# The first low word of each pair's weight sums on VectorE, and layer two's first two rows taking the sixth block together

## The chip, the core and the metric

The kernel runs on one core of a Trainium2 chip. Five engines work side by side, each through its own instructions in a fixed order: PE (TensorE, the matrix multiplications), DVE (VectorE), ACT (ScalarE), POOL (GpSimd) and SP (SyncE, which issues the transfers). An instruction that waits holds up all that stand behind it on its engine. The metric is the device time in microseconds; lower is better.

## What is computed

A block-sparse attention feeds two feed-forward layers over 1536 tokens of width 512:

```python
x = attention(q, k, v)                                # (1536, 512)
h = np.maximum(np.maximum(x @ w1, x @ w2), x @ w3)    # w1..w3: (512, 768)
y = h @ w_out                                         # layer two
out = ((y @ w_a) * (y @ w_b)) @ w_out2                # layers three and four, inner width 1536
```

## The kernel before

**Numbers in two words.** Each fp32 operand of a large product is held as a high and a low word: ACT rounds it to the high word (L464 for weights, L536 for data), and another engine subtracts that from the original to get the low word (L465, L537). A product then takes three matrix multiplications (`mm3`, L529 to L533): high by high, low by high, high by low, all 128 x 128 by 384 tokens.

**Chunks and stages.** The tokens are four chunks of 384 (c = 0 to 3). Chunks 0 and 1 go through layers one and two while the attention still runs. Chunks 2 and 3 go through layer one in `pair1`: the first two and the last of its nine steps are plain products (`plain`, names `ph`), and the six between are computed for both chunks at once by seven block products in place of eight (`products`, names `hb`, `hg`, `hd`). That scheme needs sums of weight blocks, which `w_sums` (L613) makes for a pair (f, m): POOL adds high and low word back together (L614, `rc`), DVE forms four sums in `sums4` (L471 to L474, `s12` and `s34`), and both go through `w_parts`, where ACT makes the high and one engine the low word. Before, POOL makes both low words, since `LO_G` is True. Layer two (`layer2`, names `py`) multiplies the six blocks f of h by one weight column block m for each of four rows of y. Layers three and four follow (`qb`, `qg`, `qd`, then `po`); the first products of layer three are the start of `layer3` for `order34[0]` and `order34[1]`.

**PSUM.** The products from `pair1` on share a ring of eight PSUM banks (tag "r"). A bank is taken again only when its last reader has read it, and within the seven products a bank that has been read for an intermediate result is added to afterwards, so that PE also waits for these readers: `result` (L631: DVE L633, L635, L640, ACT L638 and L684) and, in layer three, DVE L803 and L809 (`ca`, `t`) and ACT L793.

**Weights of layers three and four.** Their 512 KB pieces are loaded by SP into three buffers (`w64`). The first three loads are held back by a one-column copy on POOL (L433). From each piece ACT makes two parts (L454 into `psw` or in place, L456), DVE puts the fp32 number together (L458, L459, `w32`), POOL adds the last bits (L460), and then come the sums and splits as above (L471 to L474, L464, L465). A piece's POOL instruction frees its buffer for the next load.

**What sets the order.** The Python code says what depends on what and in which order it is written; a planner then places each engine's instructions by its own estimate of when they can run. A change in the code moves instructions on several engines, far from the lines that were edited.

Of the kernel before, what the change touches and what calls it, by code (L numbers as in the profile page):

```python
# [19 lines left out]
P = 128  # L20
# [16 lines left out]
NCH, MAXT = len(CHUNKS), max(SIZES)  # L37
# [5 lines left out]
N1, N2, NK = 3 * FF1 // P, FF1 // P, FF2 // P // 3  # L43
# [16 lines left out]


GATE, ROOM, SUMS, EARLY34 = (2, 1), 16, (40, 43, 46, 49), 6
PLAIN, XSUMS, WSUMS, WS, PT, MAX_G, LO_G, ASK = (2, 1), (2, 4), (5, 7), 8, 7, False, True, (0, 2)
RING, LEAD, TURN, ERA0, ASKS, AHEAD, PRE, TURNS = 8, 5, (11, 2, 4), 10, (3, 4, 5, 7, 9), (4, 1), 3, ((6, N1 - 6, 6, 4, 4), (24, 34), (34, 43))


# [11 lines left out]
def attention_then_maxout_then_bilinear(ctx: ExitStack, tc: tile.TileContext, qt, kt, vt, vwin, wall, const, out):  # L78
# [4 lines left out]
    V, A, G, T = nc.vector, nc.scalar, nc.gpsimd, nc.tensor  # L83
# [339 lines left out]
    w64_t, w32_t, w_t = {}, {}, {}  # L423
# [38 lines left out]
    def w_parts(r, eng, tag="w34", n=512):  # L462
        w = w_p.tile([P, 2, n], F32R, tag=tag, name="wt", bufs=2 if n < 512 else WS if tag == "ws" else WBUFS[tag != "w"])
        A.activation(w[:, 0], r, AF.Copy)  # L464
        eng.tensor_tensor(w[:, 1], r, w[:, 0], ALU.subtract)  # L465
        return w

    def sums4(a11, a12, a21, a22):

        s12, s34 = (w32_p.tile([P, 512], F32, tag=f"s{i}", name="s", bufs=1) for i in range(2))  # L470
        V.tensor_tensor(s12[:, 0:256], a21, a22, ALU.add)  # L471
        V.tensor_tensor(s12[:, 256:512], s12[:, 0:256], a11, ALU.subtract)
        V.tensor_tensor(s34[:, 0:256], a11, a21, ALU.subtract)
        V.tensor_tensor(s34[:, 256:512], a12, s12[:, 256:512], ALU.subtract)  # L474
        return s12, s34
# [37 lines left out]
    late = []  # L513

    def flush():
        while late:
            late.pop(0)()

    def bank(name):

        return ps_m.tile([P, 512], F32, tag="m", name=name)
# [7 lines left out]
    def mm3(ps, w, o, x, first, last, more=False):  # L529

        for n, (i, j) in enumerate(((0, 0), (1, 0), (0, 1))):
            ins = T.matmul(ps, w[:, i, o:o + P], x[:, j], start=first and n == 0, stop=last and n == 2, skip_group_check=more).ins  # L532
        return ins  # L533
# [10 lines left out]
    def layers12(c):  # L544

        n_, hs, pend = CHUNKS[c][2] * P, {}, [None]
        for n in range(N1):
            f, m = divmod(n, 3)
            if m == 0:
                hs[f] = hg_p.tile([P, 2, MAXT * P], F32R, tag="hg", name="hg")  # L550
            ps = bank("ph")[:, 0:n_]
            for k in range(4):
                mm3(ps, w_t[n], k * P, x_t[c, k], k == 0, k == 3)
            flush()

            def evac(f=f, m=m, ps=ps, ht=hs[f]):
                prev, pend[0] = pend[0], temp(f"t{m}", c)
                if m == 0:
                    mark[1] = A.activation(pend[0], ps, AF.Copy).ins
                else:  # L560
                    mark[0] = V.tensor_tensor(pend[0], ps, prev, ALU.max).ins
                    if m == 2:
                        split(ht, pend[0], G)

            late.append(evac)
            yield
        yield from layer2(c, hs, bank)

    def layer2(c, hs, bank):

        ys[c] = y_p.tile([P, 4, MAXT * P], F32, tag="y", name="y", bufs=NCH)
        for m in range(4):
            ps = bank("py")[:, 0:MAXT * P]
            for f in range(N2):
                if m == 0 and f == N2 - 1:
                    flush()
                mm3(ps, w_t[N1 + f], m * P, hs[f], f == 0, f == N2 - 1)
            flush()
            late.append(lambda m=m, ps=ps: halves(c, m, ps))
            yield  # L580

    xs = {}

# [25 lines left out]
    def w_sums(f, m):  # L609

        w0, w1 = (w_t[3 * (f + i) + m] for i in range(2))
        r0, r1 = (w32_p.tile([P, 512], F32, tag="rc", name="rc", bufs=2) for _ in range(2))
        for r, w in ((r0, w0), (r1, w1)):  # L613
            G.tensor_tensor(r, w[:, 0], w[:, 1], ALU.add)  # L614
        s12, s34 = sums4(*(r[:, o:o + 256] for r in (r0, r1) for o in (0, 256)))
        eng = G if LO_G else V
        s12, s34 = (w_parts(x, eng, "ws") for x in (s12, s34))
        w_s[f, m] = {"A11": (w0, 0), "A12": (w0, 256), "A22": (w1, 256),
                     "S1": (s12, 0), "S2": (s12, 256), "S3": (s34, 0), "S4": (s34, 256)}

# [2 lines left out]
    def pair1():  # L623
# [42 lines left out]
        def products(two, ahead):  # L666
# [3 lines left out]
            for i in range(7):  # L670
                for u, (f, m) in enumerate(two):
                    w, y, name = PRODUCTS[i]
                    first = (u, name) not in ps
                    if first:
                        ps[u, name] = ring(f"h{name}")
                    (wt, o), to = w_s[f, m][w], ps[u, name]
                    for k in range(2):
                        mm3(to, wt, o + k * P, operand(y, k), first and k == 0, k == 1, not first)
                    flush()

                    def evac(i=i, u=u, f=f, to=to):
                        if i < 3:
                            kept[u, i] = t = half(("s1", "m5", "u2")[i])
                            mark[1] = A.activation(t, to, AF.Copy).ins  # L684
                        elif i == 3:
                            result(f, 2, to, kept[u, 0])
                        elif i == 4:
                            result(f + 1, 3, to, kept[u, 1])
                        elif i == 5:
                            result(f, 3, to, kept[u, 2])  # L690
                        else:
                            result(f + 1, 2, to)

                    late.append(evac)
                    if u == 1 and i in ASK and ahead:
                        with behind_marks():
                            w_sums(*ahead.pop(0))
                    yield
# [5 lines left out]
        for f, m in order[:PLAIN[0]]:  # L704
            for _ in plain(f, m, lambda name: bank(name)[:, 0:MAXT * P]):
                step += 1
                with behind_marks():
                    if step in XSUMS:
                        x_sums(XSUMS.index(step))
                    elif step in WSUMS:  # L710
                        w_sums(*ahead.pop(0))
                yield
        while len(fast) - len(ahead) < 2:
            with behind_marks():
                w_sums(*ahead.pop(0))
# [4 lines left out]
        for c in (2, 3):  # L720
            yield from layer2(c, hs[c], ring)
# [4 lines left out]
    def halves(c, m, ps):  # L726

        A.activation(ys[c][:, m], ps, AF.Copy)
        if c == 3:
            sums_of(c, m, m % 2, m % 2 + 1)  # L730
        elif c == 2 and m % 2:
            sums_of(c, m)

    def sums_of(c, m, k0=0, k1=2):

        b, j = divmod(c, 2)
        (b11, b21), (b12, b22) = ((y[:, k0:k1], y[:, 2 + k0:2 + k1]) for y in (ys[2 * b], ys[2 * b + j]))

        def op(name, src):
            names = next(x for x in (("B11", "B21"), ("T1", "T2", "T3", "B22", "T4")) if name in x) if b == 0 else (name,)  # L740
            if name == names[0] and k0 == 0:
                both[b, names] = t_p.tile([P, len(names), 2, 2, MAXT * P], F32R, tag=names[0] + str(b), name="yt", bufs=1)
            ops[b, name] = t = both[b, names][:, names.index(name)]
            A.activation(t[:, 0, k0:k1], src, AF.Copy)
            V.tensor_tensor(t[:, 1, k0:k1], src, t[:, 0, k0:k1], ALU.subtract)  # L745

        def diff(tag, x, y):
            t = y_p.tile([P, k1 - k0, MAXT * P], F32, tag=f"{tag}{b}{k0 * (tag == 't1')}", name="yd")
            V.tensor_tensor(t, x, y, ALU.subtract)  # L749
            return t  # L750

        if j == 0:
            op(("B11", "B21")[m // 2], (b11, b21)[m // 2])
        elif m < 2:
            t1 = sums[b, k0] = diff("t1", b12, b11)
            op("T1", t1)
        else:
            t2 = diff("t2", b22, sums[b, k0])
            op("T2", t2)
            op("T3", diff("t3", b22, b12))  # L760
            op("B22", b22)
            op("T4", diff("t4" if b else "t3", b21, t2))
# [143 lines left out]
    for i, _ in enumerate(pair1()):  # L906
        with behind_marks():
            weights(1)
            if i in SUMS:
                m = SUMS.index(i)  # L910
# [60 lines left out]
```

## Time and profile before

| | |
|---|---|
| median of 3 runs | 550.29 us (549.81 to 550.38) |
| the profiled execution | 549.45 us |
| its span, first to last instruction | 547.2 us |
| PE busy | 534.0 us (98%) |
| DVE busy | 422.2 us (77%) |
| POOL busy | 245.9 us (45%) |
| granted TensorE clock | 1.00 throughout |

The busy share of PE includes the overlap of pipelined multiplications, so it does not show short losses; those are found in the timeline, from the starts of consecutive multiplications and from the idle time that stands in brackets behind an instruction, with the engine that ended it. The profiled execution took 2.25 us more than its span.

### The profile page before, as it was taken

How to read it: one execution, taken by the hardware profiler on the slowest of the kernel's cores; microseconds unless marked ns; L12 is line 12 of the kernel's file. 1: busy time of each engine (PE TensorE's matmuls, PEld its weight loads, DVE VectorE, ACT ScalarE, POOL GpSimd, SP SyncE). 2: the span in 40 equal slices, each digit the busy share in tenths (PEclk: the TensorE clock that was granted, in tenths of full speed). 3: DMA queues.
4: the chain of work that ended last, by engine and by line, in shares of the span. 5: the costliest groups of instructions: out<-in, count | busy, mean ns of one | idle time of the engine just before them, and what ended most of it. 6: DMA issues, size and time to landing. Idle time of an engine off the chain costs nothing.

```text
span 547.2 us, 9042 instructions
## 1 busy us (share of the span) xinstructions
PE 534.0 (98%) x3328; PEld 506.3 (93%) x3328; DVE 422.2 (77%) x863; ACT 284.6 (52%) x692; POOL 245.9 (45%) x207
## 2 busy tenths in 40 slices
PE   7899999999999999999989999999999999999997
PEld 7789999999999999989989989989998998998986
DVE  5798985885439677699999997985997798574464
ACT  4699775676533342567667645633544543340130
POOL 3479997642239577544334342521621442230120
PEclk9999999999999999999999999999999999999999
DMA  8998334375100000232311241132122121000014
GB/s 297 356 278 294 123 116 151 110 223 165 38 1 1 2 0 1 106 97 107 116 48 68 78 153 40 40 115 78 38 78 78 40 77 40 1 0 1 0 49 183
DMA packets 17132, 51.82 MB, mean 95 GB/s; under 512 B 2112, under 2 KB 2752, under 8 KB 17088
## 3 DMA queue, kind: packets, MB, share of 16 engines
q1 hardware_dynamic: 17088, 51.25, 28.0%
q8 instruction: 26, 0.43, 0.3%
q14 instruction: 18, 0.15, 0.1%
HBM read 48.09 MB, written 3.15 MB: 94 GB/s over the span
## 4 chain that ended last, share of the span: by engine, by line
PE 80%; DVE 9%; POOL 4%; issue 2%; ACT 1%; DMA 1%; DVEq 0%; POOLq 0%; ACTq 0%
PE ph L532 17%; PE qb L532 16%; PE py L532 9%; PE qg L532 8%; PE po L843 6%; PE po L844 6%; PE po L842 6%; PE qd L532 4%; PE ps L261 3%; PE psv L318 2%; PE pst L299 2%; POOL wt L465 1%; DVE yt L745 1%; DVE yd L749 1%; DVE w L459 1%
## 5 line engine op out<-in xcount | busy, mean ns | idle before, releaser
L460 POOL TENSOR_TENSOR w<-w,w 128x512 int32<-128x512 int32 x60 | 85.3, 1431 | 140.5 <-DVE w L459 79.9
L532 PE MATMUL qb<-yt,wt 128*128 128x384 f32 x576 | 109.9, 336 | 1.7 <-DVE ca L803 1.3
L532 PE MATMUL ph<-x,wt 128*128 128x384 f32 x576 | 107.2, 338 | 0.0
L532 PEld LDWEIGHTS qb<-yt,wt 128*128 128x128 f32 x576 | 101.0, 188 | 3.5 <-DVE ca L803 1.6
L532 PEld LDWEIGHTS ph<-x,wt 128*128 128x128 f32 x576 | 99.1, 188 | 0.3
L810 POOL TENSOR_TENSOR t<-t,ca 128x384 f32<-128x384 f32 x36 | 43.7, 1226 | 67.5 <-DVE t L809 67.3
L532 PE MATMUL qg<-yt,wt 128*128 128x384 f32 x288 | 57.8, 335 | 0.5 <-DVE yt L745 0.5
L856 DVE TENSOR_TENSOR acc<-po,acc 128x512 f32<-128x512 f32 (+1 forms) x61 | 40.7, 678 | 22.3 <-PE po L844 22.2
L843 PE MATMUL po<-wt,hg 128*128 128x512 f32 (+1 forms) x146 | 56.6, 387 | 0.0
L844 PE MATMUL po<-wt,hg 128*128 128x512 f32 (+1 forms) x146 | 56.5, 387 | 0.0
L842 PE MATMUL po<-wt,hg 128*128 128x512 f32 (+1 forms) x146 | 56.5, 387 | 0.0
L532 PE MATMUL py<-hg,wt 128*128 128x384 f32 x288 | 54.0, 340 | 1.1 <-DVE pt L640 1.1
L532 PEld LDWEIGHTS qg<-yt,wt 128*128 128x128 f32 x288 | 50.6, 188 | 0.8 <-DVE yt L745 0.8
L532 PEld LDWEIGHTS py<-hg,wt 128*128 128x128 f32 x288 | 49.5, 188 | 1.6 <-DVE pt L640 1.4
L536 ACT ACTIVATE hg<-t 128x384 fp32r<-128x384 f32 x60 | 30.8, 521 | 34.7 <-POOL t L810 28.7
L268 ACT ACTIVATE s<-s,nm 128x120 f32<-128x120 f32 x96 | 36.9, 387 | 20.5 <-DVE nm L267 20.4
L456 ACT ACTIVATE w<-w 128x512 int32<-128x512 uint32 x60 | 39.4, 671 | 4.7 <-DMA w<-wall 4.7
L454 ACT ACTIVATE w<-w 128x512 f32<-128x512 f32 x30 | 20.3, 675 | 41.2 <-DMA w<-wall 41.1
L464 ACT ACTIVATE wt<-w 128x512 fp32r<-128x512 f32 (+1 forms) x60 | 34.7, 583 | 12.9 <-POOL w L460 11.9
L286 POOL TENSOR_TENSOR s<-s,r 128x720 f32<-128x720 f32 x16 | 22.2, 1390 | 42.6 <-DVE r L284 36.0
L465 DVE TENSOR_TENSOR wt<-w,wt 128x512 fp32r<-128x512 f32 (+1 forms) x44 | 33.7, 768 | 1.5 <-ACT wt L464 1.3
L537 DVE TENSOR_TENSOR hg<-t,hg 128x384 fp32r<-128x384 f32 x48 | 34.2, 722 | 0.9 <-ACT hg L536 0.8
(115 smaller groups left out, 990.1 us busy)
## 6 DMA issues: line engine op xcount, KB each, us to landing
w<-wall SPq DMA_DIRECT2D x60, 512.0 KB, 3.4
qv<-qt SPq DMA_DIRECT2D x15, 384.0 KB, 6.1
row<-kt SPq DMA_DIRECT2D x8, 416.0 KB, 3.6
full<-vt SPq DMA_DIRECT2D x8, 384.0 KB, 6.2
out<-acc SPq DMA_DIRECT2D x11, 256.0 KB, 2.0
qv<-vwin SPq DMA_DIRECT2D x12, 192.0 KB, 5.3
qv<-vwin SPq DMA_DIRECT2D x12, 96.0 KB, 5.0
qv<-qt SPq DMA_DIRECT2D x1, 256.0 KB, 4.5
```

What stands on the lines that cost most here:

```text
L268: A.activation(s[:, a], s[:, a], AF.Exp, bias=nm[:, a:a + 1], scale=-1.0, accum_out=sm[:, a:a + 1])
L456: A.activation(lw.bitcast(I32), lw, AF.Copy, scale=2.0 ** -29)
L460: G.tensor_tensor(w.bitcast(I32), w.bitcast(I32), lw.bitcast(I32), ALU.add)
L464: A.activation(w[:, 0], r, AF.Copy)
L465: eng.tensor_tensor(w[:, 1], r, w[:, 0], ALU.subtract)
L532: ins = T.matmul(ps, w[:, i, o:o + P], x[:, j], start=first and n == 0, stop=last and n == 2, skip_group_check=more).ins
L537: ins = eng.tensor_tensor(dst[:, 1], src, dst[:, 0], ALU.subtract).ins
L810: G.tensor_tensor(t, t, cs[c, f], ALU.mult)
L842: T.matmul(ps, g[:, 0], w[:, 0], start=(f == 0), stop=False)
L843: T.matmul(ps, g[:, 0], w[:, 1], start=False, stop=False)
L844: ins = T.matmul(ps, g[:, 1], w[:, 0], start=False, stop=(f == 1)).ins
L856: V.tensor_tensor(acc[c, i][:, cols_], ps, acc[c, i][:, cols_], ALU.add)
```

## The change

`w_sums` makes the low word of `s12` (the blocks S1 and S2) on VectorE and that of `s34` on GpSimd; the switch `LO_G` goes. In `layer2`, for chunks 2 and 3, rows 0 and 1 are multiplied by the blocks f = 0 to 4 first, in two banks, and then both by f = 5; rows 2 and 3 and all rows of chunks 0 and 1 stay as they were. In this code's line numbers all that follows `layer2` stands three or four lines later.

```diff
-PLAIN, XSUMS, WSUMS, WS, PT, MAX_G, LO_G, ASK = (2, 1), (2, 4), (5, 7), 8, 7, False, True, (0, 2)
+PLAIN, XSUMS, WSUMS, WS, PT, MAX_G, ASK = (2, 1), (2, 4), (5, 7), 8, 7, False, (0, 2)
...
-        for m in range(4):
-            ps = bank("py")[:, 0:MAXT * P]
-            for f in range(N2):
-                if m == 0 and f == N2 - 1:
+        for ms in ((0, 1), (2,), (3,)) if c > 1 else ((0,), (1,), (2,), (3,)):
+            banks = []
+            for m in ms:
+                banks.append(bank("py")[:, 0:MAXT * P])
+                for f in range(N2 - 1):
+                    mm3(banks[-1], w_t[N1 + f], m * P, hs[f], f == 0, False)
+                if m == 0:
                     flush()
-                mm3(ps, w_t[N1 + f], m * P, hs[f], f == 0, f == N2 - 1)
-            flush()
-            late.append(lambda m=m, ps=ps: halves(c, m, ps))
-            yield
+            for m, ps in zip(ms, banks):
+                mm3(ps, w_t[N1 + N2 - 1], m * P, hs[N2 - 1], False, True)
+                flush()
+                late.append(lambda m=m, ps=ps: halves(c, m, ps))
+                yield
...
-        eng = G if LO_G else V
-        s12, s34 = (w_parts(x, eng, "ws") for x in (s12, s34))
+        s12, s34 = w_parts(s12, V, "ws"), w_parts(s34, G, "ws")
```

The engines' orders agree up to the first low word of a sum and again from the first rows of layer four on. Three places between, in the planner's order, follow; the numbers behind the names tell buffers apart.

POOL, in the last third of `pair1`, up to the copies that let the loads for layer three start (`w64`). Before:

```order
L614 TENSOR_TENSOR rc_2708<-wt_1071 128x512
L465 TENSOR_TENSOR wt_2668<-s_2662,wt_2668 128x512
L614 TENSOR_TENSOR rc_2709<-wt_1201 128x512
L465 TENSOR_TENSOR wt_2671<-s_2663,wt_2671 128x512
L537 TENSOR_TENSOR hg_2752<-pt_2749,hg_2752 128x384
L537 TENSOR_TENSOR hg_2773<-pt_2770,hg_2773 128x384
L465 TENSOR_TENSOR wt_2718<-s_2712,wt_2718 128x512
L537 TENSOR_TENSOR hg_2794<-pt_2791,hg_2794 128x384
L465 TENSOR_TENSOR wt_2721<-s_2713,wt_2721 128x512
L537 TENSOR_TENSOR hg_2814<-pt_2812,hg_2814 128x384
L433 CAST w64_2817<-hg_2637 128x1
L433 CAST w64_2820<-hg_2637 128x1
```

The same place after the change:

```order
L618 TENSOR_TENSOR rc_2708<-wt_1071 128x512
L618 TENSOR_TENSOR rc_2709<-wt_1201 128x512
L465 TENSOR_TENSOR wt_2671<-s_2663,wt_2671 128x512
L537 TENSOR_TENSOR hg_2752<-pt_2749,hg_2752 128x384
L465 TENSOR_TENSOR wt_2721<-s_2713,wt_2721 128x512
L537 TENSOR_TENSOR hg_2773<-pt_2770,hg_2773 128x384
L537 TENSOR_TENSOR hg_2794<-pt_2791,hg_2794 128x384
L537 TENSOR_TENSOR hg_2814<-pt_2812,hg_2814 128x384
L433 CAST w64_2817<-hg_2637 128x1
L433 CAST w64_2820<-hg_2637 128x1
```

The splits of the first sum (`wt_2668`, `wt_2718`) are gone from POOL, and the four `rc` additions stand together. DVE has these two splits after the change, each behind the four sums of its pair.

PE, at the start of layer two for chunk 2: `py_3119` is row 0, `py_3166` (after: `py_3140`) row 1, `py_3197` row 2; `hg_3067` is the fifth block of h, the first that the last plain products give. Before, from the first four blocks of row 2 on:

```order
L532 MATMUL py_3197<-hg_2578,wt_1291 128x384 x3
L532 MATMUL py_3197<-hg_2637,wt_1333 128x384 x3
L532 MATMUL py_3197<-hg_2752,wt_1378 128x384
L532 MATMUL py_3119<-hg_3067,wt_1562 128x384 x2
L532 MATMUL py_3166<-hg_3067,wt_1562 128x384 x2
L532 MATMUL py_3197<-hg_2752,wt_1378 128x384 x2
L532 MATMUL py_3119<-hg_3067,wt_1562 128x384
L532 MATMUL py_3166<-hg_3067,wt_1562 128x384
L532 MATMUL py_3197<-hg_2814,wt_1465 128x384 x3
L532 MATMUL py_3197<-hg_3067,wt_1562 128x384 x3
L532 MATMUL py_3220<-hg_2578,wt_1291 128x384 x3
```

After, from the first use of `hg_3067` on; rows 0 and 1 have taken the first four blocks just ahead of this, in both orders:

```order
L532 MATMUL py_3119<-hg_3067,wt_1562 128x384 x2
L532 MATMUL py_3140<-hg_3067,wt_1562 128x384 x2
L532 MATMUL py_3197<-hg_2578,wt_1291 128x384 x3
L532 MATMUL py_3119<-hg_3067,wt_1562 128x384
L532 MATMUL py_3140<-hg_3067,wt_1562 128x384
L532 MATMUL py_3197<-hg_2637,wt_1333 128x384 x3
L532 MATMUL py_3197<-hg_2752,wt_1378 128x384 x3
L532 MATMUL py_3197<-hg_2814,wt_1465 128x384 x3
L532 MATMUL py_3197<-hg_3067,wt_1562 128x384 x3
```

Rows 0 and 1 take the fifth block seven multiplications sooner, before row 2 has begun.

DVE, at the start of layer three, around `ca_3413`, which reads the bank `qb_3351` that PE then adds to; `w32_3495` and `w32_3506` are two pieces of weights. Before:

```order
L458 TENSOR_SCALAR w32_3506<-w64_3502 128x512
L459 SCALAR_TENSOR_TENSOR w32_3495<-w64_3491,w32_3495 128x512
L459 SCALAR_TENSOR_TENSOR w32_3506<-w64_3502,w32_3506 128x512
L803 TENSOR_TENSOR ca_3413<-qb_3351,m5_3388 128x384
L803 TENSOR_TENSOR ca_3421<-qg_3373,u2_3397 128x384
L465 TENSOR_TENSOR wt_3510<-w32_3495,wt_3510 128x512
L471 TENSOR_TENSOR s_3669<-w32_3506 128x256
L473 TENSOR_TENSOR s_3670<-w32_3495,w32_3506 128x256
```

After:

```order
L459 SCALAR_TENSOR_TENSOR w32_3495<-w64_3491,w32_3495 128x512
L748 TENSOR_TENSOR yt_3348<-yd_3369,yt_3348 128x384
L458 TENSOR_SCALAR w32_3506<-w64_3502 128x512
L459 SCALAR_TENSOR_TENSOR w32_3506<-w64_3502,w32_3506 128x512
L465 TENSOR_TENSOR wt_3510<-w32_3495,wt_3510 128x512
L471 TENSOR_TENSOR s_3669<-w32_3506 128x256
L473 TENSOR_TENSOR s_3670<-w32_3495,w32_3506 128x256
L806 TENSOR_TENSOR ca_3413<-qb_3351,m5_3388 128x384
```

`ca_3413` and `ca_3421` stood ahead of the split `wt_3510` and the sums `s_3669`, `s_3670`; `ca_3413` now stands behind them. On PE, 546 multiplications of 384 columns stand between the first product of sums in `pair1` and the one that adds to `qb_3351` behind `ca_3413` before the change, and 552 after it.

## Rows read from the trace of the kernel before

**Rows 1.** the page, part 1: busy us (share of the span) x instructions of each engine

```profile
PE 534.0 (98%) x3328; PEld 506.3 (93%) x3328; DVE 422.2 (77%) x863; ACT 284.6 (52%) x692; POOL 245.9 (45%) x207
```

**Rows 2.** timeline of PE, 165 to 290 us: start, us, what, [idle before <-releaser]

```profile
184.88 0.33 PE L532 MATMUL hg<-xs,wt 128*128 128x384 f32 x1
...
191.47 2.24 PE L532 MATMUL hd<-x,wt 128*128 128x384 f32 x12
193.55 0.33 PE L532 MATMUL hg<-x,wt 128*128 128x384 f32 x1
...
221.73 0.44 PE L532 MATMUL hg<-xs,wt 128*128 128x384 f32 x1 [0.40 <-ACT wt L464]
...
240.64 2.25 PE L532 MATMUL py<-hg,wt 128*128 128x384 f32 x12
243.95 23.17 PE L532 MATMUL py<-hg,wt 128*128 128x384 f32 x132 [1.06 <-DVE pt L640]
...
285.21 2.38 PE L532 MATMUL qb<-yt,wt 128*128 128x384 f32 x12 [1.31 <-DVE ca L803]
```

**Rows 3.** line L465 alone, 200 to 290 us: count, ns min/median/max, first and last start

```profile
L465 POOL TENSOR_TENSOR wt<-s,wt x6: 1283/1524/1610, 200.6 to 224.2; 128x512 fp32r<-128x512 f32 x6
L465 DVE TENSOR_TENSOR wt<-s,wt x6: 676/679/680, 249.7 to 279.1; 128x512 fp32r<-128x512 f32 x6
```

**Rows 4.** timeline of POOL, 158 to 290 us, same columns

```profile
206.50 3.77 POOL L614 TENSOR_TENSOR rc<-wt 128x512 f32<-128x512 f32 x3
...
223.27 1.02 POOL L537 TENSOR_TENSOR hg<-pt,hg 128x384 fp32r<-128x384 f32 x1
...
226.44 1.16 POOL L433 COPY w<-hg 128x1 f32<-128x1 f32 x3
...
264.47 5.29 POOL L460 TENSOR_TENSOR w<-w,w 128x512 int32<-128x512 int32 x2 [5.53 <-DVE w L459]
...
284.22 2.89 POOL L460 TENSOR_TENSOR w<-w,w 128x512 int32<-128x512 int32 x2 [5.97 <-DVE w L459]
```

**Rows 5.** timeline of DVE, 158 to 290 us, same columns

```profile
209.06 1.49 DVE L471 TENSOR_TENSOR s<-rc 128x256 f32<-128x256 f32 x1 [5.15 <-POOL rc L614]
...
222.07 1.21 DVE L640 TENSOR_TENSOR pt<-hb,pt 128x384 f32<-128x384 f32 x2
...
231.47 0.69 DVE L458 TENSOR_SCALAR w<-psw 128x512 uint32<-128x512 uint32 x1 [1.88 <-ACT psw L454]
...
243.35 0.55 DVE L640 TENSOR_TENSOR pt<-hb,pt 128x384 f32<-128x384 f32 x1
...
268.52 1.52 DVE L471 TENSOR_TENSOR s<-w 128x256 f32<-128x256 f32 x1 [1.21 <-POOL w L460]
...
282.27 0.41 DVE L458 TENSOR_SCALAR w<-w 128x512 uint32<-128x512 uint32 x1
282.60 0.55 DVE L745 TENSOR_TENSOR yt<-yd,yt 128x384 fp32r<-128x384 f32 x1
283.07 0.41 DVE L458 TENSOR_SCALAR w<-w 128x512 uint32<-128x512 uint32 x1
283.41 1.28 DVE L459 SCALAR_TENSOR_TENSOR w<-w,w 128x512 uint32<-128x512 uint32 x2
284.61 0.54 DVE L803 TENSOR_TENSOR ca<-qb,m 128x384 f32<-128x384 f32 x1
...
286.54 1.12 DVE L465 TENSOR_TENSOR wt<-w,wt 128x512 fp32r<-128x512 f32 x1 [0.92 <-ACT wt L464]
287.58 0.41 DVE L471 TENSOR_TENSOR s<-w 128x256 f32<-128x256 f32 x1
```

**Rows 6.** timeline of ACT, 222 to 290 us, same columns

```profile
230.81 0.63 ACT L454 ACTIVATE psw<-w 128x512 f32<-128x512 f32 x1 [3.92 <-DMA w<-wall]
...
285.87 0.63 ACT L464 ACTIVATE wt<-w 128x512 fp32r<-128x512 f32 x1 [2.52 <-POOL w L460]
```

**Rows 7.** line L460 alone, 200 to 290 us, columns as in rows 3

```profile
L460 POOL TENSOR_TENSOR w<-w,w x10: 1306/1344/4022, 234.3 to 285.8; 128x512 int32<-128x512 int32 x10
```

## The prediction

> **What bounds the kernel now.** The page comes first: PE is busy for 98% of the span [rows 1], so a change pays only by what PE loses between multiplications. The timeline of PE shows where that is. Twelve multiplications of 384 columns start 2.08 us apart in all (191.47 to 193.55), 0.1733 us each [rows 2]; whatever two starts lie further apart than their count times this is lost. The two orders differ only from about 185 us to the start of layer four, so I sum that stretch. From 184.88 to 285.21 are 546 multiplications, 94.6 us at that pace, in 100.3 us: 5.7 us lost, and no change in this stretch can gain more. They fall in three parts [rows 2]: 1.7 us up to 240.64 (312 multiplications; the largest is a wait for a high word from ACT at 221.73), 1.2 us at the second row of layer two (12 from 240.64, then the wait that ends at 243.95, for DVE's L640), and 2.8 us from there to 285.21 (222 multiplications), of which 1.3 us is the wait for DVE's `ca` that ends there. Behind 285.21 I count PE as fed without a gap, so a delay there goes to the end one for one. What the waits name is DVE, and it is DVE's order that I follow.
>
> **The splits.** Six low words leave POOL, at 1.28 to 1.61 us each, and come to DVE, where the same form takes 0.68 us [rows 3]; back to back an instruction there starts about 0.07 us before the end shown of the last, so 0.60 us of its queue. In the last third of `pair1` POOL's `rc` additions before start at 206.50 [rows 4] and the sums wait for the second of them until 209.06 [rows 5]. With the splits of the pair before off POOL's queue I put that second addition at 207.7, from 1.4 us less queue (one split). From there to the end of the two L640 at 222.07 + 1.21 DVE took 14.2 us [rows 5]; with two splits more, 1.2 us, and two POOL instructions less to stand behind, for which I take 0.4 us off, it ends at 222.7, hardly sooner. POOL's gain is larger: it then has only hg splits left, 1.0 us each [rows 4], and no weight split between them. The read that frees the first of the last three stands three instructions of 0.47 us ahead of DVE's end, at 221.3; ACT's high word comes between (0.55 us, by the 0.63 of a wider one [rows 6]), and three splits from 221.85 end at 224.85, where the copies that release the loads started at 226.44 [rows 4]. So the loads start 1.6 us sooner; with DVE a half to one us off either way, 0.4 to 2.3 us.
>
> PE's losses up to 240.64 I take from 1.7 to 1.1 us: the wait at 221.73 goes, since the first low word no longer stands behind hg splits on POOL, and a wait of about half a us comes at the last product of the third pair, whose DVE read now stands behind the first weights of layer three: those come with the loads (ACT at 230.81 waited 3.9 us for the load [rows 6], DVE at 231.47 behind it [rows 5]; both minus 1.6).
>
> **The two rows of layer two.** The wait at 243.95 is for the bank that L640 reads at 243.35 [rows 2, 5], 11.9 us behind the first weight instruction at 231.47. That distance stays within half a us either way (two more reads stand in it, 0.9 us, and fill an idle 0.7 us there), so the wait now ends near 242.5, a gain of 1.4 us at this place. Taking the fifth block seven multiplications sooner, 1.2 us, can cost between nothing and 1.2 us of new wait for it; I write nothing, because the next term swallows either.
>
> **Layer three.** DVE is the bound here: from 231.47 to the L459 at 283.41 its one long gap is the 1.21 us at 268.52 [rows 5]. The first of the two L459 ends at 284.0. Of the 86 instructions in this stretch, 84 are the same after the change. Two come in (an L633 and an L635 of `pair1`, 0.9 us, most of it into idle time: plus 0.25), two go behind it (an L458 of 0.33 us and a yt of 0.47 [rows 5]: minus 0.8). With the loads 1.6 us sooner this L459 ends at 284.0 - 1.6 + 0.25 - 0.8 = 281.8.
>
> Before, `ca_3413` came 0.6 us after, ran to 285.15 and released PE at 285.21. Now it stands behind a split that waits for ACT, and ACT for POOL. The price from rows: yt, L458 and the other L459, 0.47 + 0.33 + 0.60 = 1.4 us, during which POOL does not get its turn (before, it started its addition at 284.22, but two took 2.89 us where one needs 1.31 [rows 4, 7], and ACT could follow only at 285.87 [rows 6], which is 1.26 us after the last L459 of the run had gone at 284.61); then that addition, 1.25; ACT's high word, 0.63; DVE's split, 1.12 as at 286.54, since POOL's next addition stands in its way as it did there [rows 5]; two sums, 0.34 each; `ca`, 0.54; 0.1 us for the hand-overs. Sum 5.7 us, so PE goes on at about 281.8 + 5.7 + 0.05 = 287.55. It has then done six multiplications more than at 285.21, 1.04 us. **Net: 287.55 - 1.04 - 285.21 = 1.3 us later.** The 1.4 us won at layer two and the half us of `pair1` are lost here, because PE waits for DVE anyhow. Against the execution's own 549.45 us that is 550.75; the runs' median lies 0.84 us above this execution, so 551.6.
>
> Ends of this term: the loads 0.4 or 2.3 us sooner give +2.5 and +0.6. The 1.21 us gap and the stretched L471 at 268.52 (1.52 where 0.41 is usual [rows 5]) come of POOL's additions being kept out by DVE: two from 264.47 took 5.29 us [rows 4]. If DVE's new order leaves a turn for POOL sooner, up to 2.3 us go.
>
> **A rule against the trace.** The row: one L460 took 4.02 us where 1.34 is the middle [rows 7], and that one stood beside some six DVE instructions back to back. The Trainium skill (SBUF — State Buffer, "SBUF: two separate sides") says that VectorE and GpSimd share a port pair as an exclusive lock, held by whichever instruction starts first for that instruction, while the other blocks. By that rule POOL would get its turn after one DVE instruction, the 5.7 us would be 4.7 and the sum +0.3; the trace agrees on the blocking (the L471 of 1.49 us at 209.06 [rows 5]) and not on the single instruction.
>
> **Rivals.** First, POOL gets its turn behind the first of the three DVE instructions, after 0.47 us in place of 1.4: about 1.0 us less, +0.3, 550.6, no change. For it: POOL's addition at 284.22 began while the second L459 still ran [rows 4, 5]. Against it: the 4.02 us. Second, faster: POOL's turn near 264 comes early, because two reads of y in DVE's new order wait for ACT just there, and the 2.3 us at 268.52 go; with the loads 2.3 us sooner the L459 ends at 278.8, PE goes on at 284.55, net -1.7 us, 548.6. It decides at an L459 that ends before 279.4, where the net passes -1.1. Against it: what frees DVE at one place has to survive several loads and ACT rounds that stand between. Third, slower still: ACT stands behind a load before it can round the fifth block or the reads of `qb_3351`; beyond +2.5 us, 552.8 and more. That the change does not do what it says is out: the orders show the six splits on DVE and the new rows of layer two.
>
> **How the numbers follow.** About 0.2%, 1.1 us, is what a measurement of this kernel can tell from no change. The forecast (+1.3, own range +0.3 to +2.5) has 0.43, of which 0.33 lies above 1.1 us and 0.10 below. The first rival has 0.29, all within. The second has 0.22, faster. The third has 0.06, slower. So faster 0.22, same 0.39, slower 0.39. The range reaches from the second rival, 548.6, to the far end of the forecast's own, 552.9; what it leaves out is the part of the second rival that gains more, some 0.1, and the third.
>
> **What would show it.** Right: the wait for DVE at layer two's second row ends between 242 and 243; the copies on POOL start near 224.9; PE waits over 2 us in the first products of layer three, released by DVE's `ca`, and goes on at 287 to 288. Wrong: no such wait there, `ca` done before 285.5, or a copy start at 226 or later; or PE losing time behind 290, where I count none.

## The result

The changed kernel takes 553.24 us (median of 5 runs, 552.37 to 554.87) where the kernel before takes 550.13 (549.81 to 550.38): 1.0057 times as long, with a 95% interval of 1.0045 to 1.007. It is slower by more than the 0.2% that can be told, on the side to which the forecast of 551.6 us pointed, and 0.34 us beyond the range. The profiled execution took 553.11 us with a span of 551.2, 4.0 us above the span before.

The page of the changed kernel, part 1 (columns as in [rows 1]):

```profile
PE 534.3 (97%) x3328; PEld 506.3 (92%) x3328; DVE 430.5 (78%) x869; ACT 283.5 (51%) x692; POOL 235.1 (43%) x201
```

Six instructions have gone from POOL to DVE, as the counts say: 207 to 201, and 863 to 869. DVE is busy 8.3 us longer. Six splits of 0.68 us are 4.1 us; the other half is DVE's instructions getting longer.

PE's timeline, where it lost time, and first the two waits of before that [rows 2] leave out (start, us, what, [idle before <-releaser]):

```profile
216.15 1.33 PE L532 MATMUL hb<-xs,wt 128*128 128x384 f32 x6 [0.25 <-DVE pt L633]
...
272.64 0.44 PE L532 MATMUL qg<-yt,wt 128*128 128x384 f32 x1 [0.49 <-DVE yt L745]
```

The changed kernel:

```profile
185.28 0.33 PE L532 MATMUL hg<-xs,wt 128*128 128x384 f32 x1
...
215.87 1.33 PE L532 MATMUL hb<-x,wt 128*128 128x384 f32 x6 [0.27 <-DVE pt L636]
...
221.30 1.16 PE L532 MATMUL hg<-xs,wt 128*128 128x384 f32 x5 [0.17 <-DVE wt L465]
...
234.66 2.35 PE L532 MATMUL hb<-xs,wt 128*128 128x384 f32 x12 [0.76 <-DVE pt L636]
...
245.80 23.21 PE L532 MATMUL py<-hg,wt 128*128 128x384 f32 x132 [1.49 <-DVE pt L643]
...
271.80 1.32 PE L532 MATMUL qg<-yt,wt 128*128 128x384 f32 x6 [1.75 <-ACT y L731]
...
290.30 1.31 PE L532 MATMUL qb<-yt,wt 128*128 128x384 f32 x6 [2.28 <-DVE ca L806]
```

The six waits in brackets are 6.72 us where the five of before ([rows 2] and the two above) are 3.51. PE goes on behind `ca_3413` at 290.30 instead of 285.21; with six multiplications more done (1.04 us) that is 4.05 us late. Of these, 0.40 were there at the first product of sums (185.28 against 184.88), ahead of anything that the change moves; 3.65 us are the change's. Behind 290 PE shows no wait, so they go to the end.

### The profile page after: what moved, and what is told of

Read it like the earlier page. It is cut to its first block, busy times and chain, and to the rows that moved or that the text cites. A ratio compares the mean times of both kernels' runs of the same rounds, so it can differ in the third digit from the quotient of the medians.

```text
span 551.2 us, 9052 instructions
## 1 busy us (share of the span) xinstructions
PE 534.3 (97%) x3328; PEld 506.3 (92%) x3328; DVE 430.5 (78%) x869; ACT 283.5 (51%) x692; POOL 235.1 (43%) x201
## 4 chain that ended last, share of the span: by engine, by line
PE 75%; DVE 16%; ACT 2%; POOL 2%; issue 1%; DMA 1%; DVEq 0%; ACTq 0%
PE ph L532 17%; PE qb L532 16%; PE qg L532 8%; PE po L846 6%; PE po L847 6%; PE po L845 6%; PE py L532 5%; PE qd L532 4%; PE ps L261 3%; DVE wt L465 2%; PE psv L318 2%; DVE yt L748 2%; PE pst L299 2%; DVE pt L638 2%; DVE yd L752 1%; DVE pt L636 1%
## 5 line engine op out<-in xcount | busy, mean ns | idle before, releaser
L460 POOL TENSOR_TENSOR w<-w,w 128x512 int32<-128x512 int32 x60 | 85.1, 1425 | 140.2 <-DVE w L459 71.4
L859 DVE TENSOR_TENSOR acc<-po,acc 128x512 f32<-128x512 f32 (+1 forms) x61 | 40.7, 678 | 21.2 <-PE po L847 21.0
L465 DVE TENSOR_TENSOR wt<-w,wt 128x512 fp32r<-128x512 f32 (+1 forms) x44 | 36.4, 828 | 4.7 <-ACT wt L464 4.5
L537 DVE TENSOR_TENSOR hg<-t,hg 128x384 fp32r<-128x384 f32 x48 | 35.4, 749 | 1.2 <-ACT hg L536 1.1
```

Source lines behind the costliest of these rows:

```text
L460: G.tensor_tensor(w.bitcast(I32), w.bitcast(I32), lw.bitcast(I32), ALU.add)
L537: ins = eng.tensor_tensor(dst[:, 1], src, dst[:, 0], ALU.subtract).ins
L859: V.tensor_tensor(acc[c, i][:, cols_], ps, acc[c, i][:, cols_], ALU.add)
```

## Experiments

Each kernel was timed beside the kernel before on the same chip, whose median there was 550.40 to 550.45 us. "Goes on" is the multiplication that waits for `ca_3413`. Times within a stage are counted from the first product of sums, which stands at 184.4 to 187.3 us, because executions differ by some tenths of a us before it.

**Theory:** `ca_3413` stands on DVE behind a split that waits for ACT, which waits for POOL, and PE waits for `ca_3413`. **Rivals:** the rows of layer two and a new wait for ACT's read of y; or simply that DVE has more work than time, so that no order of it helps.

### One part of the change at a time

The splits alone:

```diff
-        for ms in ((0, 1), (2,), (3,)) if c > 1 else ((0,), (1,), (2,), (3,)):
...
+        for m in range(4):
+            ps = bank("py")[:, 0:MAXT * P]
+            for f in range(N2):
```

> The splits alone: the low words of s12 on DVE, those of s34 on POOL; layer two as before. Here ca_3413 stands on DVE behind the split wt_3510 and the two sums, as in the changed kernel. Theory (the place of ca_3413 behind a split that waits for POOL and ACT costs the time): PE waits about 2 to 3 us for ca in the first products of layer three and goes on at 289 to 290.5; 552.3 to 553.5 us. Rival (the rows of layer two and the new waits for ACT's read of y behind them cost it): this kernel has none of these, so 549.6 to 550.9 us.

Measured: 554.70 us, 1.0079 (1.0067 to 1.0091). PE waits 2.35 us for `ca` and goes on at 292.15, which is 104.9 us into the stretch; the changed kernel stands at 105.0. So from there on the splits alone do all that the change does. The median lies 1.2 us above the expectation. In the profiled run (555.15 us) the stretch begins 2.0 us late, at 187.27, since the clock had fallen twice in the first 30 us (last section); the other four runs were below full clock as well (0.997), but where it fell in them no trace shows. By the wait and its place the theory held, and the rival fell.

The rows alone:

```diff
-        s12, s34 = w_parts(s12, V, "ws"), w_parts(s34, G, "ws")
+        s12, s34 = w_parts(s12, G, "ws"), w_parts(s34, G, "ws")
```

> The two rows of layer two alone; both low words on POOL as before. Here ca_3413 stands ahead of the split, right behind the second L459, as in the kernel before. Theory (place of ca_3413): the wait for ca is at most 1.5 us and ends before 286.5; 549.3 to 551.0 us. Rival (rows of layer two and the waits for y): a wait for ACT of 1 to 2 us near 271 as in the changed kernel, and 551.5 to 553 us.

Measured: 552.11 us, 1.0033 (1.0022 to 1.0045), 1.7 us above the kernel before. Both missed: the time lies in the rival's range, but its wait for ACT near 271 is not there; the wait for `ca` is small, as the theory had it, but ends at 287.97, behind two waits for reads by ACT. Timelines of POOL, ACT, DVE and PE of this kernel:

```profile
278.31 4.44 POOL L460 TENSOR_TENSOR w<-w,w 128x512 int32<-128x512 int32 x1 [10.13 <-DVE w L459]
```

```profile
282.79 0.63 ACT L464 ACTIVATE wt<-w 128x512 fp32r<-128x512 f32 x1 [3.65 <-POOL w L460]
283.32 0.47 ACT L796 ACTIVATE s<-qb 128x384 f32<-128x384 f32 x1
```

```profile
281.18 0.41 DVE L458 TENSOR_SCALAR w<-w 128x512 uint32<-128x512 uint32 x1
```

```profile
283.85 1.31 PE L532 MATMUL qb<-yt,wt 128*128 128x384 f32 x6 [0.58 <-ACT s L796]
285.77 1.34 PE L532 MATMUL qb<-yt,wt 128*128 128x384 f32 x6 [0.61 <-ACT u L796]
287.97 1.31 PE L532 MATMUL qb<-yt,wt 128*128 128x384 f32 x6 [0.87 <-DVE ca L806]
```

POOL's addition begins at 278.31 and ends at 282.75, 1.2 us after DVE's run of instructions ends at 281.59: while DVE went on without a gap, POOL did not get on. ACT's high word waits for it 3.65 us, and the read of `qb` that PE needs stands behind that high word. It is the chain of the theory (DVE's run, POOL, ACT, DVE) with another reader caught in it, and the third rival of the prediction but for what ACT stands behind: POOL, and not a load.

Only chunk 2 with its rows in a pair:

```diff
-        for ms in ((0, 1), (2,), (3,)) if c > 1 else ((0,), (1,), (2,), (3,)):
+        for ms in ((0, 1), (2,), (3,)) if c == 2 else ((0,), (1,), (2,), (3,)):
```

> The changed kernel with the pair of rows in layer two for chunk 2 only; chunk 3 goes row by row as before. ca_3413 stands behind the split, as in the changed kernel. Theory: the same 2 to 2.5 us of wait for ca, 552.3 to 553.8 us; the wait of 1.75 us for ACT's read of y near 271 may go, but only lets PE come to the wait for ca sooner. Rival (the wait for y is the loss, and comes of chunk 3's pair): that wait is below 0.7 us and the time 550.6 to 551.8 us.

Measured: 554.54 us, 1.0072 (1.0055 to 1.0089). PE's timeline:

```profile
270.21 1.31 PE L532 MATMUL qg<-yt,wt 128*128 128x384 f32 x6 [0.67 <-ACT y L731]
...
289.81 2.29 PE L532 MATMUL qb<-yt,wt 128*128 128x384 f32 x6 [2.35 <-DVE ca L806]
```

The wait for y shrinks from 1.75 to 0.67 us and PE comes to `ca` that much sooner, to wait there just as long: 104.8 us into the stretch against 105.0. The wait for y costs nothing by itself. The two runs at full clock took 552.51 and 552.88 us, as the theory had it; in the other four the clock had fallen, in the profiled one toward the end of this wait (last section).

### ca_3413 ahead of the split

The split `wt_3510` (piece N12 + 8) and the sums of the next piece are held behind `ca_3413`, which is called a pin below; the second kernel has the last line alone.

```diff
-        eng.tensor_tensor(w[:, 1], r, w[:, 0], ALU.subtract)
+        with behind_all(*after):
+            eng.tensor_tensor(w[:, 1], r, w[:, 0], ALU.subtract)
...
-            w = w_parts(w32_t[q], eng)
+            w = w_parts(w32_t[q], eng, after=CA if q == N12 + 8 else ())
...
-            s12, s34 = sums4(a11, a12, a21, a22)
+            with behind_all(*(CA if q == N12 + 9 else ())):
+                s12, s34 = sums4(a11, a12, a21, a22)
...
-                            V.tensor_tensor(t, to, x, ALU.add)
+                            marks["ca", n, b, f, j] = V.tensor_tensor(t, to, x, ALU.add).ins
...
-PLAIN, XSUMS, WSUMS, WS, PT, MAX_G, ASK = (2, 1), (2, 4), (5, 7), 8, 7, False, (0, 2)
+PLAIN, XSUMS, WSUMS, WS, PT, MAX_G, ASK = (2, 1), (2, 4), (5, 7), 8, 6, False, (0, 2)
```

> The changed kernel with one thing more: the split wt_3510 and the sums s_3669 and s_3670 are held behind ca_3413 on DVE; to make room for the buffers that this holds longer, the pool of the intermediate results pt has six buffers in place of seven. Theory: ca_3413 follows the second L459 at once, so 1.2 to 1.4 us behind the first one's end instead of 5.7; PE goes on at 285.5 to 287 in place of 290.3; 549.3 to 550.8 us. Rival (DVE has more work than its time allows, and an order only shifts where PE waits): the wait for ca shrinks, but PE waits as much longer for the weights or sums that now come later, behind 290; 552.3 to 553.6 us.

> The changed kernel with six buffers of pt in place of seven and nothing else, as a control for the one before. Both theories expect 552.4 to 554.2 us; if it is faster than that, what the kernel with ca_3413 ahead gains is not the place of ca_3413, and if slower, that gain is larger than it shows.

Measured: 551.31 us (1.0018, 1.001 to 1.0027) with `ca_3413` ahead; 554.39 us (1.0076, 1.0061 to 1.0091) with six buffers alone. So the place of `ca_3413` is worth 1.9 us against the changed kernel and 3.1 against its own control; two of the control's six runs were below full clock (0.994 and 0.997), and the four at full clock took 552.8 to 555.0 us. DVE's timeline of the changed kernel, and of the one with `ca_3413` ahead:

```profile
283.91 0.68 DVE L459 SCALAR_TENSOR_TENSOR w<-w,w 128x512 uint32<-128x512 uint32 x1
284.51 0.55 DVE L748 TENSOR_TENSOR yt<-yd,yt 128x384 fp32r<-128x384 f32 x1
284.98 0.42 DVE L458 TENSOR_SCALAR w<-w 128x512 uint32<-128x512 uint32 x1
285.44 1.68 DVE L459 SCALAR_TENSOR_TENSOR w<-w,w 128x512 uint32<-128x512 uint32 x1
287.26 1.84 DVE L465 TENSOR_TENSOR wt<-w,wt 128x512 fp32r<-128x512 f32 x1
289.03 0.41 DVE L471 TENSOR_TENSOR s<-w 128x256 f32<-128x256 f32 x1
...
289.70 0.55 DVE L806 TENSOR_TENSOR ca<-qb,m 128x384 f32<-128x384 f32 x1
```

```profile
285.32 1.69 DVE L459 SCALAR_TENSOR_TENSOR w<-w,w 128x512 uint32<-128x512 uint32 x1
286.93 0.55 DVE L810 TENSOR_TENSOR ca<-qb,m 128x384 f32<-128x384 f32 x1
287.40 0.54 DVE L810 TENSOR_TENSOR ca<-qg,u 128x384 f32<-128x384 f32 x1
287.87 1.15 DVE L468 TENSOR_TENSOR wt<-w,wt 128x512 fp32r<-128x512 f32 x1
```

`ca_3413` starts 2.8 us sooner, and the split that now stands behind it ends at 289.02 instead of 289.10: it had been waiting for ACT and POOL anyway, and two reads fit into that wait. PE's timeline shows 18 multiplications in a row there:

```profile
285.64 3.28 PE L536 MATMUL qb<-yt,wt 128*128 128x384 f32 x18
```

The theory held, by the mechanism and within half a us by the time. The rival, that the loss would come back behind 290, fell for this order: one wait of 0.23 us is all that stands there.

The same with layer two row by row:

> As the run with ca_3413 ahead (split and sums of that stage behind ca_3413, six buffers of pt), but layer two as before: only the low words of s12 go to DVE. Theory: with ca_3413 ahead there is no wait for it above 0.3 us, and the splits alone then cost about as much as the changed kernel with ca_3413 ahead, 550.6 to 551.8 us. Rival (the rows of layer two cost something of their own, as they did alone): 549.6 to 550.5 us.

Measured: 551.61 us, 1.002 (1.0008 to 1.0033), as the theory said: once `ca_3413` stands ahead, the rows cost nothing and bring nothing that these runs can tell (0.3 us). What is left of the loss is 0.9 to 1.2 us; in the kernel with the rows the largest waits left are those up to layer two (0.89, 1.45 and 1.46 us) and the one for y (1.12).

### Does the same pay in the kernel before?

One kernel holds both L459 behind `ca_3413` there, the other the one of `w32_3506` alone (`q in (N12 + 9,)`); the `marks` line is as above:

```diff
-        V.scalar_tensor_tensor(w.bitcast(U32), hw, 0x80000000, w.bitcast(U32), ALU.bitwise_and, ALU.bitwise_or)
+        with behind_all(*([("ca", 0, 0, 1, 1)] if q in (N12 + 8, N12 + 9) else ())):
+            V.scalar_tensor_tensor(w.bitcast(U32), hw, 0x80000000, w.bitcast(U32), ALU.bitwise_and, ALU.bitwise_or)
```

> The kernel before with one thing more: both L459 of the pieces w32_3495 and w32_3506 are held behind ca_3413 on DVE, so that it no longer waits for them. Theory (each instruction ahead of ca_3413 on DVE is paid by PE one for one): the wait of 1.31 us for ca shrinks to below 0.3 us, 549.0 to 549.6 us. Rival (DVE has more work than its time allows, and an order only shifts where PE waits): the 1.2 us come back as a wait for the weights or sums behind 287, 550.1 to 551.0 us.

> The kernel before with the second L459 alone (of w32_3506) behind ca_3413; the first, of w32_3495, stays ahead. Theory (what may stand behind ca is what POOL cannot take up yet; POOL is busy with the first piece): PE's wait for ca falls from 1.31 to about 0.7 us and nothing comes back, 549.6 to 550.3 us. Rival (every delay of the chain L459, POOL, ACT, split comes back later, as it did with both L459 behind ca): 551 to 552.5 us.

Measured: 552.35 us (1.004, 1.0027 to 1.0053) and 552.84 us (1.0042, 1.0029 to 1.0054). Both theories missed by 2 to 3 us, and the rivals missed too (the second by 0.3 us), since more came back than was taken away. In the second, the wait for `ca` fell to 0.70 us as expected, and waits of 1.01 and 1.31 us came up behind 300. PE's timeline of the first of the two:

```profile
283.94 3.65 PE L533 MATMUL qb<-yt,wt 128*128 128x384 f32 x18
...
305.67 2.36 PE L533 MATMUL qd<-yt,wt 128*128 128x384 f32 x12 [0.39 <-DVE t L810]
313.87 0.49 PE L845 MATMUL po<-wt,hg 128*128 128x512 f32 x1 [0.50 <-DVE hg L538]
318.47 2.35 PE L533 MATMUL qb<-yt,wt 128*128 128x384 f32 x12 [0.55 <-DVE ca L804]
```

The wait for `ca` is gone, and 1.44 us of new ones stand behind 300, where before has none. Neither L459 waits for another engine in the kernel before: held back, it holds back POOL's addition, ACT's high word and the split, which ends at 289.82 where it ended at 287.66 (286.54 + 1.12, [rows 5]); 0.44 us of this is a later start of the stretch. The pins also moved instructions of the planner's order behind them, on all engines but POOL in the first kernel; which of these cost the rest stays open.

### Which low word, and what sets the loads

```diff
-        s12, s34 = w_parts(s12, V, "ws"), w_parts(s34, G, "ws")
+        s12, s34 = w_parts(s12, G, "ws"), w_parts(s34, V, "ws")
```

> The changed kernel with the two low words changed over: those of s34 on DVE, those of s12 on POOL. On DVE ca_3413 then stands behind three sums and the split of wt_3510. Theory: PE waits over 2 us for ca in the first products of layer three, 552.3 to 554 us. Rival (it is the first low word of each pair on DVE, ahead of the reads that release the loads, that makes the loads late): the copies on POOL start over 0.7 us sooner than in the changed kernel and the time is 550.3 to 551.8 us.

Measured: 553.92 us, 1.0074 (1.005 to 1.0098), as the theory said, with 2.62 us of wait for `ca`. Rows of POOL and of DVE (the stretch begins at 185.32):

```profile
226.01 0.43 POOL L433 COPY w<-hg 128x1 f32<-128x1 f32 x3
```

```profile
230.32 0.69 DVE L458 TENSOR_SCALAR w<-psw 128x512 uint32<-128x512 uint32 x1 [2.08 <-ACT psw L454]
...
282.15 0.68 DVE L459 SCALAR_TENSOR_TENSOR w<-w,w 128x512 uint32<-128x512 uint32 x1
...
287.19 0.43 DVE L471 TENSOR_TENSOR s<-w 128x256 f32<-128x256 f32 x1 [2.48 <-POOL w L460]
...
288.80 0.55 DVE L806 TENSOR_TENSOR ca<-qb,m 128x384 f32<-128x384 f32 x1
```

The rival's copies came, 0.7 us sooner, but not its time. Counted from the start of the stretch, the copies stand 0.7 us, the first L458 1.5 us and the end of the first L459 1.8 us ahead of the changed kernel (40.7, 45.0 and 97.5 against 41.4, 46.5 and 99.3). So the L459 followed the loads here; it did not with six buffers of pt alone (next section). But `ca` ends 6.5 us behind that L459, since DVE idles 2.48 us for POOL, and PE goes on 104.1 us into the stretch, 0.9 us sooner only. Against that stands the clock, which was below full speed in all six runs (0.994 to 0.997, last section).

With `ca_3413` ahead as well, with the rows and without (pt keeps its seven buffers in both):

> The low words of s34 on DVE and those of s12 on POOL, layer two's pairs of rows as in the changed kernel, and the split wt_3510 and the sums behind ca_3413. Theory (the order around ca_3413 costs 2 to 3 us whichever low word is on DVE): PE waits at most 0.3 us for ca, and the time is 2 to 3 us below that of the same kernel without the pin, so 550.9 to 551.9 us. Rival (DVE's work comes due elsewhere): 552.3 us or more, with new waits behind 290.

> As the one before, with layer two row by row as in the kernel before. Theory: the loads start 0.9 us sooner than in the kernel before, ca_3413 makes no wait, and what is left is the wait near 222 for ACT's high word and the one at layer two: 550.2 to 551.4 us. Rival (the rows of layer two save PE time at their own place): 1 us or more above the run with the rows.

Measured: 553.22 us (1.0055, 1.004 to 1.0069) and 552.55 us (1.0036, 1.0024 to 1.0048). No wait for `ca`, as expected, but 0.7 and 1.4 us gained where 2 to 3 were expected. The second came out 0.7 us below the first, so that its theory (551.4 at most) and its rival (1 us or more above) both missed. PE's timeline of the one with the rows shows what came back:

```profile
292.45 0.97 PE L536 MATMUL qd<-yt,wt 128*128 128x384 f32 x4 [1.04 <-ACT ca L808]
...
314.68 0.50 PE L849 MATMUL po<-wt,hg 128*128 128x512 f32 x1 [1.25 <-DVE ca L810]
```

So the rival, which fell for the changed order, holds here: with the same pin other waits come up. The pin is worth 1.9 to 3.1 us in the two kernels with s12 on DVE, and is not a rule.

Both low words on DVE:

> The changed kernel with both low words of each pair on DVE, none on POOL. The step in question: does POOL's queue set when the second rc addition of the last pair is done? If it does, that addition ends over 1 us sooner than in the changed kernel (208.99 from a start of the stretch at 185.28, so 23.7 us into it), at 22.7 or less, and the copies before 40.4. If POOL waits there for ACT's high words of data instead, both stay within 0.5 us of 23.7 and 41.4. ca_3413 stands behind the split here too, so the time is 553 to 555.5 us by either.

Measured: 556.17 us, 1.0103 (1.0087 to 1.0118). POOL's timeline:

```profile
208.03 1.99 POOL L537 TENSOR_TENSOR hg<-pt,hg 128x384 fp32r<-128x384 f32 x2 [2.78 <-ACT hg L536]
209.97 5.21 POOL L618 TENSOR_TENSOR rc<-wt 128x512 f32<-128x512 f32 x4
```

POOL has no weight split left and idles 2.78 us for ACT's high words of data; the `rc` additions start behind these, at 209.97, and the sums read the second at 212.55. POOL's queue does not set that time. Both alternatives missed it, though: 212.55 is 25.8 us into the stretch (from 186.72), where 22.7 or 23.7 was expected, since PE itself was late by then. It had waited 0.41 us for a split of the first sums, the clock had fallen at 188.3, and at 195.34, 8.6 us into the stretch, it did what the changed kernel does at 191.34, 6.1 us into its own. The copies (228.27, 41.6 us into the stretch) stand where the second alternative had them; the time is 0.7 us above its range.

No version here beats the kernel before.

## Why the prediction was wrong

**The direction and the place were right.** One sign of being right came: PE waits over 2 us for `ca` in the first products of layer three. That this chain costs the time is shown and not only argued, since taking `ca_3413` out of it gave 1.9 to 3.1 us back. The other signs failed: PE goes on at 290.30 (287 to 288), the wait at layer two ends at 245.80 (242 to 243), and the copies start at 226.70 (224.9), which is the sign that was set for being wrong, 226 or later.

**The length of the chain came out by luck.** From the end of the first L459 to PE going on the sum had 5.7 us, and the trace has 290.30 - 284.59 = 5.71. But two of its terms missed by 0.7 us, in opposite ways. POOL and ACT in the changed kernel:

```profile
284.73 1.83 POOL L460 TENSOR_TENSOR w<-w,w 128x512 int32<-128x512 int32 x1 [3.50 <-DVE w L459]
```

```profile
286.60 0.64 ACT L464 ACTIVATE wt<-w 128x512 fp32r<-128x512 f32 x1 [2.02 <-POOL w L460]
```

POOL's addition is done at 286.56, 1.97 us behind the L459, where the sum had 1.4 us without a turn and 1.25 of addition, 2.65. The split behind ACT then holds DVE for 1.8 us (287.26 to the sum at 289.03) where the sum had 1.12: POOL's next addition stands beside it for 1.30 us, from 287.25. So most of the saving of the first rival came, and was lost again one step on.

**The step that failed is "the loads start 1.6 us sooner".** POOL's and DVE's timelines of the changed kernel:

```profile
204.47 1.99 POOL L537 TENSOR_TENSOR hg<-pt,hg 128x384 fp32r<-128x384 f32 x2 [1.05 <-ACT hg L536]
206.40 5.23 POOL L618 TENSOR_TENSOR rc<-wt 128x512 f32<-128x512 f32 x4
...
226.70 1.18 POOL L433 COPY w<-hg 128x1 f32<-128x1 f32 x3
```

```profile
208.99 1.50 DVE L471 TENSOR_TENSOR s<-rc 128x256 f32<-128x256 f32 x1 [4.69 <-POOL rc L618]
...
219.45 1.79 DVE L465 TENSOR_TENSOR wt<-s,wt 128x512 fp32r<-128x512 f32 x1
...
223.50 1.21 DVE L643 TENSOR_TENSOR pt<-hb,pt 128x384 f32<-128x384 f32 x2
...
231.79 0.69 DVE L458 TENSOR_SCALAR w<-psw 128x512 uint32<-128x512 uint32 x1 [2.39 <-ACT psw L454]
```

With the 0.40 us of late start taken off, the copies are at 226.30, 0.14 us sooner than before [rows 4], where the sum had 224.85. The 1.45 us that lack:

- 0.9: the second `rc` addition is there at 208.59, and not at 207.7. I took one split off POOL's queue, but POOL now waits 1.05 us for ACT just ahead of these additions; with every split off it, it waited 2.78 us there.
- 0.7: from there to the end of the two L643 DVE took 15.7 us, and not 15.0. The two splits more were in the sum. But the 0.4 us that I took off for two POOL instructions less did not come: beside POOL five of DVE's instructions here are 4.9 us longer together than their forms usually are, the moved split (1.79 us) among them, where before it was also five, by 4.6 us.
- from the L643 to the copies: 2.0 us, where I had 2.15.

**What the miss did behind the loads.** Less the late start, the first L459 ends at 284.19, and the sum had 281.8: 2.4 us. Of these, 1.5 are the loads (the L458 at 231.39 against 231.47 before, a gain of 0.1 and not 1.6). The other 0.9 is DVE's way from there to the L459, 52.8 us where I had 52.0: the two instructions that go behind it (0.8 us) did not shorten it. Beside POOL nine of DVE's instructions on this way are longer than usual, by 6.9 us together, where before it was six, by 4.7 us, and the 1.9 us for which DVE idled before are gone. As the chain from there kept its length, PE goes on 2.35 us later than the sum said: 1.3 + 2.35 = 3.65.

That loads 1.6 us sooner would have brought the L459 forward by as much, as the sum has it, is not shown. DVE with six buffers of pt alone, where the stretch begins at 184.43:

```profile
229.95 0.69 DVE L458 TENSOR_SCALAR w<-psw 128x512 uint32<-128x512 uint32 x1 [1.23 <-ACT psw L454]
...
283.30 0.68 DVE L459 SCALAR_TENSOR_TENSOR w<-w,w 128x512 uint32<-128x512 uint32 x1
```

The first L458 stands 1.0 us sooner in the stretch than in the changed kernel (45.5 against 46.5), but DVE idles 1.8 us on the way, and the L459 ends 0.2 us later (99.5 against 99.3). With s34 on DVE 1.5 us sooner became 1.8. So the way of 52 us from the loads to the L459, which the sum carried over with two corrections, is a second step that does not hold by itself.

**Against the median** the forecast of 551.6 misses by 1.64 us and not by 2.35, since it adds 0.84 us between execution and median that the changed kernel does not have: its profiled execution took 553.11, its median is 553.24. That is luck too.

**The terms on the way** were off, but hidden, as the prediction said for one of them. Layer two: the wait was to end at 242.5 and ended at 245.8, since it hangs on the first L458, and since the distance from there to the read that ends it, which was to stay at 11.9 us within half a us, is 13.4 (231.79 to 245.19). The products: 1.20 us of waits where I had 1.1 of losses, with the wait behind the first weights at 0.76 where I had half a us. The new wait for y near 271 I had not seen; it only delays PE's arrival at `ca`.

**The range** had the loads 0.4 us sooner as its far end, +2.5. Nothing in the rows excluded 0.1, and the stretch of DVE beside POOL had no bound of its own in it. The second rival, a faster kernel at 0.22, rested on the loads and on the 2.3 us at 268.52. Of these the gap of 1.21 us is gone, but two of DVE's instructions between 266 and 271 are now 1.1 us longer than usual where one was, so that nothing was won.

**On the rule of the Trainium skill** (SBUF — State Buffer, "SBUF: two separate sides"), by which the blocked side waits for the one instruction that holds the shared ports: the addition of 4.44 us above ended only when DVE paused, after seven DVE instructions, the one under way counted. The trace agrees again that one side blocks the other, and not that one instruction is the measure. The addition at 284.73 fits a pause as well: DVE has one of 0.04 us there, between the end of the L458 (284.98 + 0.42) and the L459 at 285.44, and by its end (286.56) and the usual 1.31 us [rows 7] the addition began to work near 285.3, an estimate.

## What to carry to other kernels

An instruction moved to another engine is paid there with what it stretches and what stretches it (here 8.3 us of busy time for 4.1 us of work), and frees its old queue only if that queue was what the next step waited for: look for idle time with a releaser just ahead of that step. A read that frees a bank can stand ahead of work that is going to wait anyway at little cost (0.23 us of new wait in one kernel here; in another more came back); put ahead of work that others wait for, it came back further on in both kernels that tried it. Where a planner sets the order, an edit of half a us moves others worth 2 to 3 us, so each part wants a run of its own.

## What the runs showed of the hardware

**The clock can fall after a wait of 1.8 us in the middle of a busy stretch.** Timeline and then windows of PE in the kernel with the splits alone and `ca_3413` ahead (busy us, granted clock, DMA share and GB/s of each half us):

```profile
236.17 3.79 PE L536 MATMUL hb<-xs,wt 128*128 128x384 f32 x12 [1.78 <-DVE pt L636]
```

```profile
236.00:236.50 0.50, 0.33 (x2) 1.00 1.05 410
236.50:237.00 0.50, 0.50 (x4) 0.69 0.61 246
237.00:237.50 0.50, 0.50 (x3) 0.50 0.03 8
...
240.00:240.50 0.50, 0.50 (x4) 0.90 0.86 213
```

PE had waited 1.78 us and gone on for about half a us when the granted clock fell to 0.50, the 1.2 GHz level, until 240. Twelve multiplications took 3.6 us, start to start, where twelve take 2.08 [rows 2]: the wait cost nearly twice itself. The same was seen after waits of 1.81 and 1.87 us for ACT's high word near 222 (s34 on DVE), toward the end of the 2.35 us for `ca` with one chunk in pairs, and after 1.85 us in the first 11 us of the splits alone. It also fell behind shorter waits: 0.40 and 0.96 us (splits alone, at 24.4) and 1.21 and 0.41 us (both low words on DVE, at 188.3). After the 2.28 us of the changed kernel's profile, after 2.35 us for `ca` with the splits alone and after 2.62 us with s34 on DVE it did not fall. The kernel before, whose longest wait behind 165 us is 1.31 us, ran at 0.999 or 1.0 in 42 of 47 later runs; of the five runs of the changed kernel two had 0.994 and 0.997, and these are its two longest. A wait has a price beyond its length, then, but not in every execution, and its median here is a run at full clock: the clock is no part of the 3.65 us.

**The profile of before was its shortest execution.** 47 later runs of it have spans of 547.3 us and more, 548.2 in the middle, against the profile's 547.2. The two pinned kernels, whose orders are those of before up to `ca`, wait 1.30 and 1.32 us for `yt` near 273, where the profile of before shows 0.49. A sum of tenths from one execution carries that much with it; the prediction put it into the 0.84 us between execution and median.
